# All four value tiles of a chunk in one stretch, with the global rows' sums in front of it

## The chip, the core and the metric

The kernel runs on one core of a Trainium2 chip. The metric is the device time of one execution in microseconds (us). The engines have short names here: PE is TensorE (matmuls), DVE VectorE, ACT ScalarE, POOL GpSimd, SP SyncE. The last one only issues DMAs in this kernel.

## The reference

A Longformer attention (a window of 32 positions on either side, and 8 global positions that see all and are seen by all) over 8 batches, 8 heads, 576 positions and 64 dimensions, and behind it a gated GELU block with a residual gate:

```python
scores = scale * np.matmul(q, k.transpose(0, 1, 3, 2))
mask = np.abs(pos[:, None] - pos[None, :]) <= 32
mask = mask | is_global[:, None] | is_global[None, :]
attn = softmax(np.where(mask, scores, -1e9))
x = np.matmul(attn, v)                 # to (4608, 512)
ffn_out = gelu(x @ w_gate) * (x @ w_val) @ w_out
return x + sigmoid(x @ w_res) * ffn_out
```

## The kernel before

The 4608 tokens are worked on in nine chunks of 512 (`c` = 0 to 8), each of eight windows of 64 queries, or four tiles of 128 tokens (`t` = 0 to 3). While chunk c goes through the gated block, chunk c+1's attention is made between its matmuls, so that PE always has work. The order is written by hand: each engine executes its instructions in the order in which the program gives them, and waits where an operand or a buffer is not ready.

For a chunk, `ffn_in` makes the 12 hidden tiles (`g_ps`, `v_ps`, `ht`). Behind them stand 16 work items, `work_f`: for each of the four token tiles a gate (`r_ps`, four matmuls, then a tanh into `rsb` on ACT) and three thirds of the output product (`f_ps`, four matmuls each). After the last third, DVE makes `prb` from `rsb` and `f_ps`, POOL adds the tokens (`ob`), and SP stores `ob`. The pieces of the next chunk's attention are hung in front of numbered work items, in `jobs`:

- `half(0)` and `half(1)` (job 0 and 3) make the scores `sc` of four windows each. ACT takes the exponentials into `pt`. The mask, a product of two bf16 tiles in SBUF (`pt` and `maskw`, line 565), is made on DVE in four instructions per half by `held_mask`.
- `global_rows` (job 3, in chunks whose successor brings a new batch, `held`) sums the global rows into the PSUM tile `sn`. DVE multiplies it by `head8` into `vgs` (line 520).
- `two(0)` and `two(2)` (job 4 and 8) make the values of two tiles: `local_values` (32 matmuls of 65 columns with 64 columns of the array, line 583), `global_values` (two matmuls per tile, each on 64 rows of the array, which read `vgs`, line 596), the normalizing on DVE (`norm`, a reciprocal and a product per tile or half tile), and `turn_x`, which for chunks above 1 is a DMA transpose from `xtok` to `xt` on SP. The next chunk's matmuls read `xt`.

PSUM has eight banks: four in the pool `psm` (`g_ps`, `v_ps`, `r_ps`, `f_ps`, the second scores), two in `pss` (the first scores), and one pair in `psn`, which is used in turn by the global scores, `sn` and a value tile. A tile that gets a bank waits until the last reader of the tile before has finished with it.

Of the kernel before, what the change touches and what calls it, by code (L numbers as in the profile page):

```python
# [8 lines left out]
F32 = mybir.dt.float32  # L9
# [4 lines left out]
ALU = mybir.AluOpType  # L14


def view(t, p0, pn, off, dims):

    step = t.ap[0][0]
    return bass.AP(tensor=t.tensor, offset=t.offset + p0 * step + off, ap=[[step, pn]] + dims)  # L20
# [3 lines left out]
def kernel(  # L24
# [12 lines left out]
    nc = tc.nc  # L37
    B, H, S, D = q.shape
# [8 lines left out]
    NW = S // 64  # L47
    CH = 8
    NCH = B * NW // CH
    NQT = 5  # L50
    VG = D + 1
    HV = 4 * VG
# [4 lines left out]
    work = ctx.enter_context(tc.tile_pool(name="work", bufs=2))  # L57
    psm = ctx.enter_context(tc.tile_pool(name="psm", bufs=4, space=bass.MemoryType.PSUM))
    pss = ctx.enter_context(tc.tile_pool(name="pss", bufs=2, space=bass.MemoryType.PSUM))
    psn = ctx.enter_context(tc.tile_pool(name="psn", bufs=1, space=bass.MemoryType.PSUM))  # L60
    ctx.enter_context(tc.manual_schedule())

    def pair_of(shape, name, dt=BF16):
        return [const.tile(shape, dt, name=f"{name}{i}", tag=f"{name}{i}") for i in range(2)]
# [7 lines left out]
    ve = [t.rearrange("p (c h e) -> p c h e", h=H, e=VG) for t in ve_flat]  # L72
    vo = [t.rearrange("p (c h e) -> p c h e", h=H, e=VG) for t in vo_flat]
    gt = pair_of([128, S + 128], "gt")
    ptg = pair_of([128, 5, 64], "ptg")
    xt = pair_of([128, NKT, 512], "xt")
    xtok = pair_of([128, 4, 512], "xtok")
    pt = const.tile([128, H, CH, 64], BF16, name="pt", tag="pt")
    vgs = const.tile([128, 2, H * VG], BF16, name="vgs", tag="vgs")
# [423 lines left out]
    def global_rows(b):  # L503

        e = b % 2
        if b:
            sn = psn.tile([128, 2, 512], F32, name="sn", tag="nd")[:, 0, 0:2 * VG]
        else:
            sn = pss.tile([128, 2 * VG], F32, name="sn", tag="sc")
        for c in range(-1, 5):  # L510
            for p in range(NP):
                if c < 0:
                    nc.tensor.matmul(sn[32 * p:32 * p + 32, :], own[e][:, 32 * p:32 * p + 32],
                                     view(vgb, 0, 128, (b // 2) * VG, [[0, 2], [1, VG]]), start=True, stop=False)
                else:
                    nc.tensor.matmul(sn[32 * p:32 * p + 16, :], ptg[e][:, c, 16 * p:16 * p + 16],
                                     ve[e][:, c, 2 * p:2 * p + 2, :], start=False, stop=(c == 4))
        n = NP if b else NP // 2
        for p in range(0, NP, n):
            nc.vector.tensor_tensor(view(vgs, 0, 128, e * H * VG + 2 * VG * p, [[2 * VG, n], [VG, 2], [1, VG]]),  # L520
                                    view(sn, 0, 128, 0, [[0, n], [VG, 2], [1, VG]]),
                                    view(head8, 0, 128, 2 * p, [[2, n], [1, 2], [0, VG]]), ALU.mult)
# [27 lines left out]
    def scores(c, quad, pps=(0, 1), between=None):  # L550

        i0 = (CH * c + 4 * quad) % NW
        banks = []
        for pp in pps:
            pool, tag = (psm, "mm") if pp else (pss, "sc")
            sc = [pool.tile([128, 2, 4, 64], F32, name="sc", tag=tag) for _ in range(2)]
            heads(c, quad, pp, sc, True)
            banks += [(pp, u, sc[u]) for u in range(2)]
        if between:
            between()  # L560
        mine = [weigh(quad, *which, stay=(c == 1)) for which in banks]

        def mask(n0, n1):
            for m, x in mine[n0:n1]:
                nc.vector.tensor_tensor(m, x, view(maskw, 0, 128, 64 * i0, [[0, 2], [64, 4], [1, 64]]), ALU.mult)  # L565
        return mask

    def split(c, t):
        return c == 0 and t % 2 == 0 or c > 1 and t % 2 == 1

    def local_values(c, t):
        if split(c, t):
            pool, tag = (pss, "sc") if c else (psm, "mm")
            nds = [pool.tile([128, 512], F32, name=f"nd{hf}", tag=tag) for hf in range(2)]
            nd = None
        else:
            nd = psn.tile([128, 2, 512], F32, name="nd", tag="nd")
            nds = [nd[:, 0, :], nd[:, 1, :]]
        wins = [divmod(CH * c + 2 * t + e, NW) for e in range(2)]
        for h in range(H):  # L580
            for e, (b, i) in enumerate(wins):
                vw = ve[b % 2][:, i // 2, h, :] if i % 2 == 0 else vo[b % 2][:, i // 2, h, :]
                nc.tensor.matmul(nds[h // 4][64 * e:64 * e + 64, VG * (h % 4):VG * (h % 4) + VG],  # L583
                                 pt[:, h, 2 * t + e, :], vw, start=(h % 4 == 0), stop=False)
        return nd, nds, wins

    def global_values(c, t, begun):
        nd, nds, wins = begun
        if wins[0][0] == wins[1][0]:
            parts = [(wins[0][0], 64 + 64 * wins[0][1])]  # L590
        else:
            parts = [(wins[0][0], S), (wins[1][0], 0)]
        for n, (b, c0) in enumerate(parts):
            for hf in range(2):
                k0, k1 = (64 * hf, 64 * hf + 64) if c > 1 else (0, 128)
                nc.tensor.matmul(nds[hf][:, 0:HV], gt[b % 2][k0:k1, c0:c0 + 128],  # L596
                                 vgs[k0:k1, b % 2, HV * hf:HV * hf + HV], start=False, stop=(n == len(parts) - 1))

    def values(c, t, begun=None):
        begun = begun or local_values(c, t)  # L600
# [3 lines left out]
    def norm(c, t, begun):  # L604
        nd, nds, wins = begun
        rden = work.tile([128, H], F32, name="rden", tag="rden")
        if split(c, t):
            for hf in range(2):
                num = nds[hf][:, 0:HV].rearrange("p (h e) -> p h e", e=VG)
                nc.vector.reciprocal(rden[:, 4 * hf:4 * hf + 4], num[:, :, D])  # L610
                nc.vector.tensor_tensor(xtok[c % 2][:, t, 256 * hf:256 * hf + 256].rearrange("p (h d) -> p h d", d=D),  # L611
                                        num[:, :, 0:D], view(rden, 0, 128, 4 * hf, [[1, 4], [0, D]]), ALU.mult)
            return
        num = nd[:, :, 0:HV].rearrange("p a (h e) -> p a h e", e=VG)
        r2 = rden.rearrange("p (a h) -> p a h", a=2)
        nc.vector.reciprocal(r2, num[:, :, :, D])
        nc.vector.tensor_tensor(xtok[c % 2][:, t, :].rearrange("p (a h d) -> p a h d", a=2, d=D),  # L617
                                num[:, :, :, 0:D], view(rden, 0, 128, 0, [[4, 2], [1, 4], [0, D]]), ALU.mult)

    def turn_x(c, t):  # L620
        mine = xt[c % 2][:, :, 128 * t:128 * t + 128]
        if c > 1:
            nc.sync.dma_start(mine, xtok[c % 2][:, t, :], transpose=True)
            return
        tx = pss.tile([128, NKT, 128], BF16, name="tx", tag="sc")
        for kk in range(NKT):
            nc.tensor.transpose(tx[:, kk, :], xtok[c % 2][:, t, 128 * kk:128 * kk + 128], ident)
        (nc.vector.tensor_copy if c or t == 3 else nc.scalar.copy)(mine, tx)
# [195 lines left out]
    for c in range(NCH):  # L824
        b = c + 1
# [5 lines left out]
        held = None  # L831
        for j in range(NFF):
# [54 lines left out]
            elif b < B:  # L887
# [15 lines left out]
                if j == 11:  # L903
                    held = global_scores(b)
        work_f = [w for t in range(4) for w in ffn_out(c, t)]
# [46 lines left out]
            continue  # L952
        jobs = {n: [] for n in range(16)}
        if c + 1 < NCH:
            if held is not None:
                jobs[3].append(lambda: global_rows(b))
            held_mask = {}

            def half(quad, between=None):
                held_mask[quad] = scores(c + 1, quad, between=between)  # L960

            jobs[0].append(lambda: half(0, held and (lambda: global_exp(b, *held))))
            jobs[1] += [gates[-1][1], lambda: held_mask[0](0, 4)]
            jobs[3].append(lambda: half(1))

            def two(t0):
                both = [local_values(c + 1, t) for t in (t0, t0 + 1)]
                for t in (t0, t0 + 1):
                    global_values(c + 1, t, both[t - t0])
                for t in (t0, t0 + 1):  # L970
                    norm(c + 1, t, both[t - t0])
                    turn_x(c + 1, t)

            jobs[4].append(lambda: two(0))
            jobs[8].append(lambda: two(2))
            jobs[5].append(lambda: held_mask[1](0, 2))
            jobs[6].append(lambda: held_mask[1](2, 4))
        for n in range(16):
            for w in jobs[n]:
                w()  # L980
# [33 lines left out]
```

## Time and profile before

| | |
|---|---|
| time, median of 3 runs | 385.8 us (385.33 to 386.08) |
| the profiled execution | 385.43 us |
| its span, first to last instruction | 383.7 us |
| PE busy | 370.2 us, 96% |
| DVE busy | 200.7 us, 52% |
| ACT busy | 169.6 us, 44% |
| POOL busy | 168.9 us, 44% |
| granted clock of PE | 1.00 |

The span leaves out what lies around the program, 1.7 us here. Busy times are added over instructions, and PE's matmuls overlap, so its 96% says only that it is seldom idle for long.

### The profile page before, as it was taken

How to read it: one execution, taken by the hardware profiler on the slowest of the kernel's cores; microseconds unless marked ns; L12 is line 12 of the kernel's file. 1: busy time of each engine (PE TensorE's matmuls, PEld its weight loads, DVE VectorE, ACT ScalarE, POOL GpSimd, SP SyncE). 2: the span in 40 equal slices, each digit the busy share in tenths (PEclk: the TensorE clock that was granted, in tenths of full speed). 3: DMA queues.
4: the chain of work that ended last, by engine and by line, in shares of the span. 5: the costliest groups of instructions: out<-in, count | busy, mean ns of one | idle time of the engine just before them, and what ended most of it. 6: DMA issues, size and time to landing. Idle time of an engine off the chain costs nothing.

```text
span 383.7 us, 8470 instructions
## 1 busy us (share of the span) xinstructions
PE 370.2 (96%) x3332; PEld 185.1 (48%) x3332; DVE 200.7 (52%) x467; ACT 169.6 (44%) x291; POOL 168.9 (44%) x203
## 2 busy tenths in 40 slices
PE   3989989999999999999999999999999999999996
PEld 2574555445544554455444544454445444444444
DVE  7767674536723573447434744564446534553322
ACT  4763685336333543355334633372338233723311
POOL 7877683868255624661366128712501210121012
PEclk9999999999999999999999999999999999999999
DMA  8999999799949943999399939994990410041002
GB/s 242 251 375 365 246 334 219 165 179 162 106 112 148 202 72 104 129 193 106 92 141 172 125 98 127 188 97 126 105 165 4 109 57 0 3 113 53 0 29 83
DMA packets 156810, 53.70 MB, mean 140 GB/s; under 512 B 140194, under 2 KB 147234, under 8 KB 156770
## 3 DMA queue, kind: packets, MB, share of 16 engines
q1 hardware_dynamic: 80832, 42.80, 46.8%
q0 software_dynamic: 75392, 9.84, 43.9%
q8 instruction: 26, 0.43, 0.5%
q10 hardware_dynamic: 546, 0.52, 0.4%
q14 instruction: 14, 0.11, 0.1%
HBM read 39.19 MB, written 9.44 MB: 127 GB/s over the span
## 4 chain that ended last, share of the span: by engine, by line
PE 84%; DMA 9%; SPq 3%; POOL 2%; issue 1%; DVE 0%; ACTq 0%; DVEq 0%; POOLq 0%
PE f_ps L703 24%; PE v_ps L647 22%; PE g_ps L647 22%; PE r_ps L673 8%; DMA extra<-in_moe_w_val_dram 5%; PE nd L583 3%; SPq L185 3%; PE sc L540 2%; DMA wo_t<-in_k_dram 2%; PE nd L596 2%; DMA xtok<-in_v_dram 2%; DMA ht<-in_q_dram 1%; POOL wo_t L145 1%; PE sg L478 1%; PE sg L485 1%
## 5 line engine op out<-in xcount | busy, mean ns | idle before, releaser
L656 DVE SCALAR_TENSOR_TENSOR ht<-gsb,v_ps 128x512 bf16<-128x512 bf16 x108 | 74.2, 688 | 97.5 <-PE v_ps L647 90.2
L653 ACT ACTIVATE gsb<-g_ps 128x512 bf16<-128x512 f32 x108 | 64.4, 597 | 121.9 <-PE g_ps L647 120.7
L709 POOL TENSOR_TENSOR ob<-prb,xtok 128x512 f32<-128x512 f32 x35 | 40.3, 1155 | 167.0 <-DVE prb L707 167.0
L647 PE MATMUL g_ps<-xt,wg_t 128*128 128x512 bf16 (+1 forms) x456 | 111.9, 368 | 0.0
L647 PE MATMUL v_ps<-xt,wv_t 128*128 128x512 bf16 (+1 forms) x456 | 111.9, 368 | 0.0
L703 PE MATMUL f_ps<-wo_t,ht 128*128 128x512 bf16 x420 | 97.9, 379 | 0.0
L647 PEld LDWEIGHTS <-wv_t 128*128 128x128 bf16 x456 | 43.5, 98 | 49.1
L647 PEld LDWEIGHTS <-wg_t 128*128 128x128 bf16 x456 | 43.4, 98 | 48.7
L703 PEld LDWEIGHTS <-ht 128*128 128x128 bf16 x420 | 40.4, 98 | 46.9
L681 ACT ACTIVATE rsb<-r_ps 128x512 bf16<-128x512 f32 x36 | 21.9, 611 | 66.5 <-PE r_ps L673 66.5
L707 DVE SCALAR_TENSOR_TENSOR prb<-rsb,f_ps 128x512 f32<-128x512 bf16 x35 | 24.1, 688 | 51.2 <-PE f_ps L703 50.4
L673 PE MATMUL r_ps<-wr_t,xt 128*128 128x512 bf16 x144 | 37.0, 381 | 1.0 <-ACT rsb L681 1.0
L547 ACT ACTIVATE pt<-sc 128x512 bf16<-128x512 f32 x64 | 33.3, 615 | 3.8 <-PE sc L540 3.8
L91 POOL DMA_DIRECT2D q_st<-in_q_dram x25 | 21.5, 866 | 18.2 <-DMA qt<-q_st 18.1
L99 POOL DMA_DIRECT2D ve<-in_v_dram x30 | 25.5, 866 | 0.0
L565 DVE TENSOR_TENSOR pt<-pt,maskw 128x512 bf16<-128x512 bf16 x56 | 21.9, 422 | 2.5 <-ACT pt L547 0.9
L91 POOL DMA_DIRECT2D k_st<-in_k_dram x25 | 21.2, 867 | 3.6 <-DMA kt<-k_st 2.9
L673 PEld LDWEIGHTS <-xt 128*128 128x128 bf16 x144 | 12.3, 98 | 15.8 <-issue 3.9
L583 PEld LDWEIGHTS <-pt 128*64 128x64 bf16 x576 | 11.2, 110 | 9.7 <-issue 5.0
L583 PE MATMUL nd<-ve,pt 128*64 128x65 bf16 x320 | 13.6, 196 | 0.7 <-DVE xtok L617 0.6
L617 DVE TENSOR_TENSOR xtok<-nd,rden 128x512 bf16<-128x512 f32 x20 | 13.8, 691 | 0.8
L611 DVE TENSOR_TENSOR xtok<-nd,rden 128x256 bf16<-128x256 f32 x32 | 13.6, 425 | 1.1
(174 smaller groups left out, 289.4 us busy)
## 6 DMA issues: line engine op xcount, KB each, us to landing
out_dram<-ob SPq DMA_DIRECT2D x35, 256.0 KB
vo<-ve SPq DMA_DIRECT2D x12, 260.0 KB
q_st<-in_q_dram POOLq DMA_DIRECT2D x20, 128.0 KB, 6.3
k_st<-in_k_dram POOLq DMA_DIRECT2D x20, 128.0 KB, 6.7
ve<-in_v_dram POOLq DMA_DIRECT2D x18, 128.0 KB, 7.6
wo_t<-in_k_dram SPq DMA_DIRECT2D x8, 256.0 KB
vraw<-in_q_dram SPq DMA_DIRECT2D x8, 256.0 KB
extra<-in_moe_w_out_dram SPq DMA_DIRECT2D x4, 512.0 KB
```

The lines of the kernel that those rows point to most:

```text
L91: nc.gpsimd.dma_start(dst[0:n, r, :].rearrange("p (h d) -> p h d", d=D), src[b].rearrange("h s d -> s h d")[128 * r:128 * r + n])
L99: nc.gpsimd.dma_start(t[p0:p1, c, :, 0:D], v[b].rearrange("h s d -> s h d")[s0 + p0:s0 + p1])
L547: nc.scalar.activation(sc if stay else mine, sc, ACTF.Exp, bias=0.0, scale=SCALE)
L565: nc.vector.tensor_tensor(m, x, view(maskw, 0, 128, 64 * i0, [[0, 2], [64, 4], [1, 64]]), ALU.mult)
L583: nc.tensor.matmul(nds[h // 4][64 * e:64 * e + 64, VG * (h % 4):VG * (h % 4) + VG], pt[:, h, 2 * t + e, :], vw, start=(h % 4 == 0), stop=F ...
L647: nc.tensor.matmul(held[what][:, c0:c1], w[:, kk, 128 * j:128 * j + 128], x[:, kk, c0:c1], start=(kk == 0), stop=(kk == NKT - 1))
L653: nc.scalar.activation(held["s"], held["g"], ACTF.Gelu, bias=0.0, scale=1.0)
L656: nc.vector.scalar_tensor_tensor(ht[:, j, :], held["s"], 0.5, held["v"], ALU.mult, ALU.mult)
L673: nc.tensor.matmul(r_ps, xt[c % 2][:, kk, 128 * t:128 * t + 128], wr_t[:, kk, :], start=(kk == 0), stop=(kk == NKT - 1))
L703: nc.tensor.matmul(held["f"], ht[:, j, 128 * t:128 * t + 128], wo_t[:, j, :], start=(j == 0), stop=(j == NFF - 1))
L707: nc.vector.scalar_tensor_tensor(prb, held["r"], 1.0, held["f"], ALU.add, ALU.mult)
L709: nc.gpsimd.tensor_tensor(ob, prb, xtok[c % 2][:, t, :], ALU.add)
```

## The change

In chunks 2 to 8 the values of all four tiles are made in one stretch, `all_values`, in front of work item 6. It uses six banks: `outer` (the `pss` pair) for tile 0, `middle` (two of `psm`) for tile 1, and `inner` (the `psn` pair) for tile 2 and three heads of each half of tile 3. The fourth head of each half of tile 3 goes to the free columns of `outer`. First come the 64 local matmuls of all tiles, then the global ones, then all the normalizing and the four transposes. `global_rows` moves from job 3 to the front of this stretch. The third gate moves from item 8 to item 5. All four masks of the second half are made in job 4, in front of the second gate.

```diff
     def split(c, t):
-        return c == 0 and t % 2 == 0 or c > 1 and t % 2 == 1
+        return c == 0 and t % 2 == 0
...
+    def all_values(c, before=None):
+
+        if before:
+            before()
+        HH = H // 2
+        H3 = HH - 1
+        outer = [pss.tile([128, 512], F32, name=f"nd0{hf}", tag="sc") for hf in range(2)]
+        middle = [psm.tile([128, 512], F32, name=f"nd1{hf}", tag="mm") for hf in range(2)]
+        inner = psn.tile([128, 2, 512], F32, name="nd2", tag="nd")
+
+        def places(t, hf):
+            if t < 3:
+                return [((outer, middle)[t][hf] if t < 2 else inner[:, hf, :], 0, 0, HH)]
+            return [(inner[:, hf, :], HV, 0, H3), (outer[hf], HV, H3, HH)]
+
+        for t in range(4):
+            for h in range(H):
+                hf, n = divmod(h, HH)
+                bank, o, h0 = [(bank, o, h0) for bank, o, h0, h1 in places(t, hf) if h0 <= n < h1][0]
+                o += VG * (n - h0)
+                for e in range(2):
+                    b, i = divmod(CH * c + 2 * t + e, NW)
+                    vw = ve[b % 2][:, i // 2, h, :] if i % 2 == 0 else vo[b % 2][:, i // 2, h, :]
+                    nc.tensor.matmul(bank[64 * e:64 * e + 64, o:o + VG], pt[:, h, 2 * t + e, :], vw,
+                                     start=(n == 0 and t < 3), stop=False)
+        for t in range(4):
+            (b, i), (b2, _) = (divmod(CH * c + 2 * t + e, NW) for e in range(2))
+            parts = [(b, 64 + 64 * i)] if b == b2 else [(b, S), (b2, 0)]
+            for n, (b, c0) in enumerate(parts):
+                for part in range(len(places(t, 0))):
+                    for hf in range(2):
+                        bank, o, h0, h1 = places(t, hf)[part]
+                        k0 = 64 * hf
+                        nc.tensor.matmul(bank[:, o:o + VG * (h1 - h0)], gt[b % 2][k0:k0 + 64, c0:c0 + 128],
+                                         vgs[k0:k0 + 64, b % 2, HV * hf + VG * h0:HV * hf + VG * h1],
+                                         start=False, stop=(t in (1, 3) and n == len(parts) - 1))
+
+        def divide(num, dst, a, n):
+            rden = work.tile([128, H], F32, name="rden", tag="rden")
+            r = rden[:, 0:a * n].rearrange("p (a h) -> p a h", h=n)
+            nc.vector.reciprocal(r, num[:, :, :, D])
+            nc.vector.tensor_tensor(dst, num[:, :, :, 0:D], view(rden, 0, 128, 0, [[n, a], [1, n], [0, D]]), ALU.mult)
...
+        for t in range(4):
+            if t == 2:
+                both(0, 0, HH, 2)
+            elif t == 3:
+                both(HV, 0, H3, 3)
+            for hf in range(2):
+                for bank, o, h0, h1 in places(t, hf):
+                    if t != 2 and (t < 3 or h0):
+                        divide(bank[:, o:o + VG * (h1 - h0)].rearrange("p (a h e) -> p a h e", a=1, e=VG),
...
+            turn_x(c, t)
...
         if c + 1 < NCH:
-            if held is not None:
-                jobs[3].append(lambda: global_rows(b))
+            work_f[5:9] = [work_f[8]] + work_f[5:8]
...
-            def two(t0):
-                both = [local_values(c + 1, t) for t in (t0, t0 + 1)]
-                for t in (t0, t0 + 1):
-                    global_values(c + 1, t, both[t - t0])
-                for t in (t0, t0 + 1):
-                    norm(c + 1, t, both[t - t0])
-                    turn_x(c + 1, t)
-
-            jobs[4].append(lambda: two(0))
-            jobs[8].append(lambda: two(2))
-            jobs[5].append(lambda: held_mask[1](0, 2))
-            jobs[6].append(lambda: held_mask[1](2, 4))
+            jobs[4].append(lambda: held_mask[1](0, 4))
+            jobs[6].append(lambda: all_values(c + 1, held and (lambda: global_rows(b))))
```

Three places show how instructions move. The first is DVE's order while chunk 3's attention is made, before the change, from the first half's masks on (`x4` are four such instructions, and in brackets stand the engines that an instruction waits for):

```order
L565 TENSOR_TENSOR pt<-pt,maskw 128x2x256 [waits Activation_49] x4
L520 TENSOR_TENSOR vgs<-sn,head_169 128x520 [waits PE_49]
L707 SCALAR_TENSOR_TENSOR prb<-rsb,f_ps 128x512 [waits PE_49,Activation_49,Pool_49]
L616 RECIPROCAL rden<-nd 128x8 [waits PE_49]
L617 TENSOR_TENSOR xtok_89<-nd,rden 128x512 [waits DVE_49]
L610 RECIPROCAL rden<-nd_2306 128x4 [waits PE_49]
L611 TENSOR_TENSOR xtok_89<-nd_2306,rden 128x256 [waits DVE_49]
```

Behind these come the second half tile's reciprocal and product, and only then the second half's four masks. DVE's order at the same place in the changed kernel:

```order
L565 TENSOR_TENSOR pt<-pt,maskw 128x2x256 [waits Activation_49] x4
L765 SCALAR_TENSOR_TENSOR prb<-rsb,f_ps 128x512 [waits PE_49,Activation_49,Pool_49]
L565 TENSOR_TENSOR pt<-pt,maskw 128x2x256 [waits Activation_49] x4
L520 TENSOR_TENSOR vgs<-sn,head_169 128x520 [waits PE_49]
L637 RECIPROCAL rden<-nd_2316 128x4 [waits PE_49]
L638 TENSOR_TENSOR xtok_89<-nd_2316,rden 128x256 [waits DVE_49]
```

The second half's masks have moved up to stand directly behind `prb`, and `vgs` has moved behind them.

The second place is PE's order in the changed kernel, around the start of chunk 2's stretch (`nd00` and `nd01` are `outer`, `nd10` is half of `middle`, `nd2` is `inner`; one row stands for each run of like matmuls):

```order
L731 MATMUL r_ps_1734<-wr_t_96,xt1_87 128x512
L731 MATMUL r_ps_1741<-wr_t_96,xt1_87 128x512
L513 MATMUL sn_1748<-vgb_232,own0_214 32x130
L516 MATMUL sn_1748<-ve0_78,ptg0_84 16x130
L620 MATMUL nd00_1774<-ve1_79,pt_90 64x65
L620 MATMUL nd10_1776<-vo0_80,pt_90 64x65
L620 MATMUL nd2_1778<-ve0_78,pt_90 64x65 [waits DVE_49]
L630 MATMUL nd00_1774<-vgs_91,gt1_83 128x260
L630 MATMUL nd2_1778<-vgs_91,gt0_82 128x195
L761 MATMUL f_ps_1881<-wo_t_95,ht_92 128x512
```

`sn` and the first matmul into `nd2`, which waits for DVE, now have only tile 0's and tile 1's 32 local matmuls between them; before, 32 score matmuls and four of `f_ps` stood there.

The third place is SP's DMA queue from the stores of chunk c's tile 0 on, before the change:

```order
L711 DMA out_dram<-ob 128x512
L623 DMA_TRANSPOSE xt_86<-xtok_88 128x4x128 x2
L711 DMA out_dram<-ob 128x512
L623 DMA_TRANSPOSE xt_86<-xtok_88 128x4x128 x2
L711 DMA out_dram<-ob 128x512 x2
```

and in the changed kernel:

```order
L769 DMA out_dram<-ob 128x512
L681 DMA_TRANSPOSE xt_86<-xtok_88 128x4x128 x4
L769 DMA out_dram<-ob 128x512 x3
```

The four transposes now stand together, ahead of tile 1's store.

## Rows read from the trace of the kernel before

**Rows 1.** Page, busy time, share and instructions of PE and others.
```profile
PE 370.2 (96%) x3332; PEld 185.1 (48%) x3332; DVE 200.7 (52%) x467; ACT 169.6 (44%) x291; POOL 168.9 (44%) x203
```

**Rows 2.** Timeline of PE, 249 to 270 us: start, length, line, tiles, count.
```profile
253.75 0.24 PE L513 MATMUL sn<-vgb,own 128*32 128x130 bf16 x4
253.82 0.46 PE L516 MATMUL sn<-ve,ptg 128*16 128x130 bf16 x20
254.21 0.64 PE L540 MATMUL sc<-qt,kt 64*128 64x64 bf16 x32
254.78 1.04 PE L703 MATMUL f_ps<-wo_t,ht 128*128 128x512 bf16 x4
255.75 0.22 PE L583 MATMUL nd<-vo,pt 128*64 128x65 bf16 x1
...
256.38 0.40 PE L596 MATMUL nd<-vgs,gt 64*128 64x260 bf16 x4
256.71 1.04 PE L673 MATMUL r_ps<-wr_t,xt 128*128 128x512 bf16 x4
257.59 2.75 PE L703 MATMUL f_ps<-wo_t,ht 128*128 128x512 bf16 x12
260.27 0.22 PE L583 MATMUL nd<-vo,pt 128*64 128x65 bf16 x1
...
262.11 2.75 PE L703 MATMUL f_ps<-wo_t,ht 128*128 128x512 bf16 x12
...
268.16 1.03 PE L647 MATMUL g_ps<-xt,wg_t 128*128 128x512 bf16 x4
```

**Rows 3.** Windows, early: length, then busy time by engine, PEclk, DMA.
```profile
52.50:54.00 1.50, 0.53 (x25) 0.41 (x18) 1.25 (x3) 1.50 (x4) 1.39 (x3) 1.00 1.04 389
```

**Rows 4.** Timeline of DVE in the same chunk.
```profile
251.86 0.46 DVE L501 TENSOR_TENSOR gt<-gt,maskr 128x576 bf16<-128x576 bf16 x1 [1.36 <-ACT gt L500]
...
254.33 0.70 DVE L520 TENSOR_TENSOR vgs<-sn,head 128x520 bf16<-128x520 f32 x1
255.95 0.69 DVE L707 SCALAR_TENSOR_TENSOR prb<-rsb,f_ps 128x512 f32<-128x512 bf16 x1 [0.93 <-PE f_ps L703]
...
258.11 0.17 DVE L610 RECIPROCAL rden<-nd 128x4 f32<-128x4 f32 x1
...
258.66 1.42 DVE L565 TENSOR_TENSOR pt<-pt,maskw 128x512 bf16<-128x512 bf16 x4
```

**Rows 5.** Timeline of DVE near the kernel's start.
```profile
16.16 0.42 DVE L765 COPY vo<-ve 64x1040 bf16<-64x1040 bf16 x1
...
18.65 1.12 DVE L501 TENSOR_TENSOR gt<-gt,maskr 128x576 bf16<-128x576 bf16 x1
19.99 0.76 DVE L520 TENSOR_TENSOR vgs<-sn,head 128x260 bf16<-128x260 f32 x2 [0.22 <-PE sn L516]
```

**Rows 6.** Timeline of PE there, with its releaser.
```profile
20.47 0.72 PE L596 MATMUL nd<-vgs,gt 128*128 128x260 bf16 x3 [0.53 <-DVE vgs L520]
```

**Rows 7.** Groups by line and shape: count, busy us, mean ns, idle.
```profile
L520 DVE TENSOR_TENSOR vgs<-sn,head 128x260 bf16<-128x260 f32 x2 | 0.8, 422 | 0.2 <-PE sn L516 0.2
...
L267 POOL CAST k_st<-wo_t 128x512 bf16<-128x512 f32 x2 | 1.2, 618 | 0.0
```

**Rows 8.** Timeline of ACT in the same chunk.
```profile
254.65 2.07 ACT L547 ACTIVATE pt<-sc 128x512 bf16<-128x512 f32 x4 [0.36 <-PE sc L540]
```

**Rows 9.** Timeline of POOL in the same chunk.
```profile
256.73 1.15 POOL L709 TENSOR_TENSOR ob<-prb,xtok 128x512 f32<-128x512 f32 x1 [6.89 <-DVE prb L707]
```

**Rows 10.** Timeline of POOL near the kernel's start.
```profile
16.37 0.69 POOL L190 CAST ve<-vraw 128x512 bf16<-128x512 f32 x1 [0.27 <-DMA vraw<-in_v_dram]
...
18.30 1.16 POOL L774 COPY vo<-ve 64x1040 bf16<-64x1040 bf16 x1
```

**Rows 11.** Timeline of SyncE's DMA queue in the same chunk.
```profile
262.88 2.53 SPq L623 DMA_TRANSPOSE xt<-xtok  x2
```

**Rows 12.** Timeline of PE in chunk 2's first values.
```profile
98.05 0.19 PE L583 MATMUL nd<-vo,pt 128*64 128x65 bf16 x1 [0.32 <-issue]
```

More of the change, by code (lines that the diff above doesn't have):

```diff
@@ L568, in split @@
     def split(c, t):
-        return c == 0 and t % 2 == 0 or c > 1 and t % 2 == 1
+        return c == 0 and t % 2 == 0
     def local_values(c, t):
         if split(c, t):
-            pool, tag = (pss, "sc") if c else (psm, "mm")
-            nds = [pool.tile([128, 512], F32, name=f"nd{hf}", tag=tag) for hf in range(2)]
+            nds = [psm.tile([128, 512], F32, name=f"nd{hf}", tag="mm") for hf in range(2)]
             nd = None
@@ L594, in global_values, with both @@
             for hf in range(2):
-                k0, k1 = (64 * hf, 64 * hf + 64) if c > 1 else (0, 128)
-                nc.tensor.matmul(nds[hf][:, 0:HV], gt[b % 2][k0:k1, c0:c0 + 128],
-                                 vgs[k0:k1, b % 2, HV * hf:HV * hf + HV], start=False, stop=(n == len(parts) - 1))
+                nc.tensor.matmul(nds[hf][:, 0:HV], gt[b % 2][:, c0:c0 + 128],
+                                 vgs[:, b % 2, HV * hf:HV * hf + HV], start=False, stop=(n == len(parts) - 1))
+    def all_values(c, before=None):
[36 more added lines that the diff above has]
+            nc.vector.tensor_tensor(dst, num[:, :, :, 0:D], view(rden, 0, 128, 0, [[n, a], [1, n], [0, D]]), ALU.mult)
+        def both(o, h0, h1, t):
+            divide(inner[:, :, o:o + VG * (h1 - h0)].rearrange("p a (h e) -> p a h e", e=VG),
+                   xtok[c % 2][:, t, :].rearrange("p (a h d) -> p a h d", a=2, d=D)[:, :, h0:h1, :], 2, h1 - h0)
+        for t in range(4):
[7 more added lines that the diff above has]
+                        divide(bank[:, o:o + VG * (h1 - h0)].rearrange("p (a h e) -> p a h e", a=1, e=VG),
+                               xtok[c % 2][:, t, :].rearrange("p (a h d) -> p a h d", a=2, d=D)[:, hf:hf + 1, h0:h1, :],
+                               1, h1 - h0)
+            turn_x(c, t)
```

## The prediction

> **What bounds the kernel now.** I read the page's busy shares first, and there TensorE (PE) is busy for 96% of the span [rows 1]. A busy share does not say that the engine works back to back, so I then went through one chunk's matmuls in order of time, in the stretch where chunk 6's attention is made between chunk 5's output products [rows 2]. The reader is to see that each group starts when the one before has streamed through. From 262.11 to 268.16, 28 matmuls of 512 columns take 6.05 us, 0.216 us each; so 4 take 0.86 and 12 take 2.59. Wherever the shape of the array changes (128\*128, 64\*128, 128\*64, 128\*32), the step is longer: 12 matmuls before the values take 257.59 to 260.27, 2.68, which is 0.09 more than 2.59, and the four gate matmuls that follow a change take 256.71 to 257.59, 0.88, another 0.01 to 0.02. I take 0.09 for a change and 0.01 for the slower restart. There is no other idle time in this stretch, so PE sets the end, and the question for each edit is what PE streams, how often it changes shape, and for whom it waits. The granted clock is 1.00 (the 2.4 GHz level), and it stayed so through a stretch of 1.5 us in which PE was busy for only 0.53 us [rows 3]; a wait of about 1 us should cost its own length and nothing for the clock.
>
> **The change, part by part.** All times below are counted from 253.75 in that chunk, which ends at 268.16, after 14.41 us.
>
> *PE without any wait.* Before, the order is sn, scores, f, values, gate, f, values, gate, f and so on. After, it is scores, f, two gates, sn, all values, f and so on. From the rows: scores to f 0.57 (254.21 to 254.78), four f matmuls behind a change 0.88, the two gates 0.86 each, one change 0.09, so sn begins at 3.26 and its larger part at 3.33. From there to the next shape is 0.39 (253.82 to 254.21), so the values begin at 3.72. 32 value matmuls and a change take 0.63 (255.75 to 256.38), so 32 alone take 0.54: tile 2 could begin at 4.26 and the global matmuls at 4.89. Two pairs of global matmuls and a change take 0.33 (256.38 to 256.71), so 0.12 a pair: three pairs 0.36, the fourth tile's four narrower ones with the same 520 columns 0.13, a change 0.09, which gives 5.47. Twelve f matmuls behind a change 2.60, then the unchanged 6.05: the chunk ends at 14.12. That is 0.29 us less than 14.41, the worth of three changes of shape, and seven chunks have it: 2.0 us. The two extra matmuls per chunk are in it.
>
> *The wait for the global rows' sums.* The new `inner` tile (value tiles 2 and 3) lies in the same bank pair as sn, so its first matmul waits until VectorE (DVE) has read sn into vgs. In this chunk vgs starts 0.51 after the larger part of sn (253.82 to 254.33) and takes 0.70 [rows 2, 4]. From DVE's end to PE's start I count 0.05: two vgs pieces begin at 19.99, the first lasts 0.42, and the waiting matmul starts at 20.47 [rows 5 to 7]. So vgs could end at 3.33 + 0.51 + 0.70 = 4.54 and PE go on at 4.59, not 4.26: 0.33 us in each of the six chunks that have new global rows. This alone eats the gain (-0.29 + 0.33 = +0.04 a chunk). Before, scores and f lay between sn and the next use of that bank, and nothing waited.
>
> *The masks.* This is where I expect the time to go. The four mask multiplications of the second half now stand directly behind prb, the product that ends tile 0's f. Before, four normalizing operations stood between, and the masks ran as 4 in 1.42 us (each 0.42 long, a new one each 0.33) at 258.66, long after ScalarE's exponentials (2.07 us, begun 0.44 after the scores) [rows 4, 8]. After, prb starts 1.17 behind f's start (254.78 to 255.95), so at 0.57 + 1.17 = 1.74, and ends at 2.43; the first mask starts 0.09 before that end, at 2.34, and ends at 2.76. The exponentials start near 0.44 and are done by 2.6, so they don't hold the masks up. Undisturbed, the masks end at 3.76, just in time for vgs at 3.84.
>
> But prb also releases GpSimd's (POOL) sum ob, 0.78 after prb's start (255.95 to 256.73), which takes 1.15 us [rows 9]: at 2.52, in the middle of the first mask. Before, ob ran beside the normalizing, which reads PSUM. The trace shows what a DVE product of two bf16 tiles in SBUF does beside a POOL operation: `gt*maskr` takes 0.46 at 251.86 [rows 4] but 1.12 at 18.65, where a POOL copy ran from 18.30 to 19.46; it ended 0.31 after that copy, so in effect it began 0.15 before the copy's end [rows 5, 10]. The reverse is there too: a POOL cast issued at 16.37 during a DVE copy (16.16 to 16.58) took 0.69 against 0.62 for its shape [rows 7], so it began 0.14 before DVE's end, ahead of DVE's next operation. By these rows ob begins at 2.76 - 0.14 = 2.62 and ends at 3.77, the second mask begins at 3.62 and ends at 4.04, the fourth ends at 4.70, vgs starts at 4.61 and ends at 5.31, and PE goes on at 5.36 instead of 4.26. That is 1.10 of waiting: +0.81 us in each of six chunks. Chunk 8 has no sn; there tile 2 could begin at 3.80 and waits for the fourth mask until 4.75: +0.66.
>
> The Trainium skill, "SBUF — State Buffer", section "Who interferes with whom", says that a DVE instruction with two SBUF inputs and a GpSimd instruction that reads SBUF exclude each other, and that whichever issues first keeps the port for its whole instruction. The trace agrees that one blocks the other, but shows an overlap of 0.14 and 0.15 us at the ends; without it, by the page, the masks would end 0.29 later and the time be 7 x 0.29 = 2.0 us longer, 393.0. I take the rows' value.
>
> *Costed at nothing.* The third gate's earlier place: it uses a bank that an exponential of the second scores has freed long before. DVE's normalizing in one burst: each half tile takes 0.55 (258.11 to 258.66), so the burst is at most 9 x 0.55 = 5.0 us, hidden under the 8.65 us of f and gate matmuls that follow the stretch; tile 1's prb comes later by that, and nothing in the chunk waits for it. The four transposes on SyncE's queue are a rival below.
>
> **Sum.** 6 x 0.81 + 0.66 = 5.5 us. The profiled execution took 385.43, so 390.9; it lies 0.37 below the median of the three runs shown (385.8), within their scatter of 0.75. I write 391.0.
>
> **The rivals.**
> *A, DVE keeps the port.* If ob has to wait until the four masks are through, the masks end at 3.76 and only the 0.33 wait stays: 6 x 0.04 - 0.28 (chunk 8, whose masks are then ready 0.01 late) = about 0, 385.4. For it: the masks follow each other closely, with no semaphore between, and no row shows POOL and the next DVE operation both asking at once. Against it: in the row at 16.37 POOL got in before DVE's next operation.
> *C, the lock bites in part.* If ob holds up the masks for half of the 0.78 us that I count (5.36 - 4.59 = 0.77 on PE), 6 x 0.43 + 0.2 = 2.8: 388.2.
> *W, the transposes are late too.* Tile 3's DMA transpose was issued 262.88 + 1.27 = 264.15, 4.0 us before the next chunk's first matmul [rows 2, 11]. After, it stands behind the burst, up to 0.2 + 5.0 us behind the stretch's end, with 8.65 us to go: 3.45 left. If a transpose needs the full 4.0, PE waits up to 0.55 in seven chunks: 3.9 on top, 394.8. No row shows a wait for it, so the need may be far less.
> *F, faster.* If vgs came before tile 2 is due, no wait at all: 7 x 0.29 = 2.0 gained, 383.4. It decides at 4.26: vgs would have to end 0.28 us earlier than the 0.51 + 0.70 of the rows, and ob must not disturb the masks. A smaller gain is a hole of 0.32 us in PE at 98.05, in chunk 2's first values, for which the trace names no releaser [rows 12]; it may go or stay, and I leave it in.
>
> **How the numbers follow.** The port's case 0.70, A 0.14, C 0.06, W 0.06, F 0.04. The likeliest gives 391.0, by itself 390.3 to 392.2 (the hole gone; vgs or the masks 0.2 us later in each chunk). The range 385.2 to 392.4 takes in A, C and nearly all of the likeliest; W, F and the page's value are left out. A measurement of this kernel tells about 0.2%, 0.77 us, from no change: faster 0.05 (F, and a little of A), same 0.13 (the rest of A), slower 0.82.
>
> **What would show it.** In the changed kernel's profile: three changes of shape fewer per chunk; a PE wait of about 1.1 us before tile 2's first value matmul, released by DVE's vgs, in six chunks, and by a mask in the seventh; among the last three of the four masks behind prb one that takes over 1 us instead of 0.42; ob of tile 0 beginning inside the first mask. If the masks all take 0.42 and ob is long instead, A holds and the wait is 0.33. Wrong altogether would be a wait in front of the first value matmuls, or one at the next chunk's first matmul, which would be W.

## The result, and the profile after

The changed kernel takes 391.7 us (median of five runs, 390.77 to 392.08) and the kernel before 385.9 (five runs beside it, 385.33 to 386.08): a ratio of 1.0137, 95% interval 1.0110 to 1.0164. By the ratio it is slower by 5.3 us, by the two medians by 5.8, and the forecast was 391.0.

The page's busy times and the group of the masks, in the profiled execution of 391.75 us (columns of the group: busy us, mean ns of one, idle time ahead of it):

```profile
PE 370.2 (95%) x3348; PEld 187.6 (48%) x3348; DVE 211.9 (54%) x495; ACT 169.3 (43%) x291; POOL 169.4 (43%) x203
...
L565 DVE TENSOR_TENSOR pt<-pt,maskw 128x512 bf16<-128x512 bf16 x56 | 28.6, 540 | 2.5 <-ACT pt L547 0.9
```

PE is busy for as long as before [rows 1], so the added time is time in which it waits. DVE gained 11 us, and 6.7 of them are in the 56 masks, which the change only moves: they took 21.9 us before, a mean of 422 ns, and 28.6 now.

Now the chunk of [rows 2] in the changed kernel, PE's timeline:

```profile
257.81 0.64 PE L540 MATMUL sc<-qt,kt 64*128 64x64 bf16 x32
258.39 1.04 PE L761 MATMUL f_ps<-wo_t,ht 128*128 128x512 bf16 x4
259.26 1.89 PE L731 MATMUL r_ps<-wr_t,xt 128*128 128x512 bf16 x8
261.08 0.24 PE L513 MATMUL sn<-vgb,own 128*32 128x130 bf16 x4
261.15 0.45 PE L516 MATMUL sn<-ve,ptg 128*16 128x130 bf16 x20
261.53 0.22 PE L620 MATMUL nd<-vo,pt 128*64 128x65 bf16 x1
...
262.05 0.19 PE L620 MATMUL nd<-ve,pt 128*64 128x65 bf16 x1
263.21 0.19 PE L620 MATMUL nd<-vo,pt 128*64 128x65 bf16 x1 [0.97 <-DVE vgs L520]
...
263.85 0.62 PE L630 MATMUL nd<-vgs,gt 64*128 64x260 bf16 x10
264.41 5.35 PE L761 MATMUL f_ps<-wo_t,ht 128*128 128x512 bf16 x24
...
273.05 1.03 PE L705 MATMUL g_ps<-xt,wg_t 128*128 128x512 bf16 x4
```

Tile 1's last local matmul starts at 262.05 and tile 2's first at 263.21. That is 1.16 where a step is 0.03 (tile 2's rows go on at 263.24), so PE waits 1.13 us, for vgs. DVE and POOL in the same place, then PE's waits over the whole span (us in total, times, longest):

```profile
259.56 0.69 DVE L765 SCALAR_TENSOR_TENSOR prb<-rsb,f_ps 128x512 f32<-128x512 bf16 x1 [1.25 <-PE f_ps L761]
260.16 0.42 DVE L565 TENSOR_TENSOR pt<-pt,maskw 128x512 bf16<-128x512 bf16 x1
...
260.16 1.71 DVE L565 TENSOR_TENSOR pt<-pt,maskw 128x512 bf16<-128x512 bf16 x2
...
260.16 2.38 DVE L565 TENSOR_TENSOR pt<-pt,maskw 128x512 bf16<-128x512 bf16 x4
262.47 0.68 DVE L520 TENSOR_TENSOR vgs<-sn,head 128x520 bf16<-128x520 f32 x1
```
```profile
260.33 1.26 POOL L767 TENSOR_TENSOR ob<-prb,xtok 128x512 f32<-128x512 f32 x1 [6.43 <-DVE prb L765]
```
```profile
PE nd L620 <- DVE vgs L520: 5.8, 6, 1.0
```

The first mask takes 0.42 and ends at 260.58; both first masks together take 1.71, so the second ends at 261.87; all four take 2.38 where they took 1.42 [rows 4]. POOL's ob was issued at 260.33, inside the first mask, and ended at 261.59. With the 1.15 that it takes alone [rows 9] it began at 260.44, 0.14 before the first mask's end, and the second mask, 0.42 long, began at 261.45, 0.14 before ob's end. The six waits are the six chunks with new global rows. Chunks (from one chunk's first `g_ps` to the next one's) last 40.28 us instead of 39.45, and the last one 38.66 instead of 38.04: +0.83 and +0.62, where the forecast was +0.81 and +0.66.

### The profile page after: what moved, and what is told of

Read it like the earlier page. It is cut to its first block, busy times and chain, and to the rows that moved or that the text cites. A ratio compares the mean times of both kernels' runs of the same rounds, so it can differ in the third digit from the quotient of the medians.

```text
span 390.1 us, 8535 instructions
## 1 busy us (share of the span) xinstructions
PE 370.2 (95%) x3348; PEld 187.6 (48%) x3348; DVE 211.9 (54%) x495; ACT 169.3 (43%) x291; POOL 169.4 (43%) x203
## 4 chain that ended last, share of the span: by engine, by line
PE 77%; DMA 10%; DVE 7%; SPq 3%; POOL 1%; issue 1%; ACTq 0%; DVEq 0%; POOLq 0%
PE f_ps L761 24%; PE g_ps L705 21%; PE v_ps L705 21%; PE r_ps L731 4%; DVE pt L565 4%; DMA qt<-in_moe_w_val_dram 2%; DMA wo_t<-in_k_dram 2%; PE sc L540 2%; DMA extra<-in_moe_w_res_dram 2%; DMA vraw<-in_moe_w_out_dram 2%; SPq L185 1%; DMA ht<-in_q_dram 1%; SPq L142 1%; DVE prb L765 1%; PE nd L620 1%; PE nd L630 1%
## 5 line engine op out<-in xcount | busy, mean ns | idle before, releaser
L761 PE MATMUL f_ps<-wo_t,ht 128*128 128x512 bf16 x420 | 96.8, 379 | 0.0
L739 ACT ACTIVATE rsb<-r_ps 128x512 bf16<-128x512 f32 x36 | 21.9, 612 | 74.3 <-PE r_ps L731 74.2
L731 PE MATMUL r_ps<-wr_t,xt 128*128 128x512 bf16 x144 | 35.7, 380 | 1.0 <-ACT rsb L739 1.0
L565 DVE TENSOR_TENSOR pt<-pt,maskw 128x512 bf16<-128x512 bf16 x56 | 28.6, 540 | 2.5 <-ACT pt L547 0.9
L638 DVE TENSOR_TENSOR xtok<-nd,rden 128x256 bf16<-128x256 f32 (+3 forms) x56 | 23.8, 424 | 2.3
L731 PEld LDWEIGHTS <-xt 128*128 128x128 bf16 x144 | 13.4, 98 | 16.1 <-issue 0.9
L637 DVE RECIPROCAL rden<-nd 128x4 f32<-128x4 f32 (+3 forms) x56 | 9.7, 174 | 9.7 <-PE nd L630 9.7
L540 PEld LDWEIGHTS <-kt 64*128 64x128 bf16 x576 | 10.0, 96 | 8.9 <-issue 8.1
L620 PE MATMUL nd<-ve,pt 128*64 128x65 bf16 x248 | 10.2, 195 | 3.9 <-DVE vgs L520 3.9
```

The lines of the kernel that those rows point to most:

```text
L638: nc.vector.tensor_tensor(dst, num[:, :, :, 0:D], view(rden, 0, 128, 0, [[n, a], [1, n], [0, D]]), ALU.mult)
L731: nc.tensor.matmul(r_ps, xt[c % 2][:, kk, 128 * t:128 * t + 128], wr_t[:, kk, :], start=(kk == 0), stop=(kk == NKT - 1))
L761: nc.tensor.matmul(held["f"], ht[:, j, 128 * t:128 * t + 128], wo_t[:, j, :], start=(j == 0), stop=(j == NFF - 1))
```

## The experiments

All are timed against the kernel before on the same chip. "Chunk" is the length of a regular chunk, "last" that of the chunk beside which chunk 8's attention is made, "wait" PE's wait in front of or among tile 2's local matmuls in a regular chunk, all from the profiled executions.

| kernel | median us | ratio (95% interval) | chunk | last | wait |
|---|---|---|---|---|---|
| before | 385.4 to 385.9 | 1 | 39.45 | 38.04 | 0 |
| after | 391.7 | 1.0137 (1.0110 to 1.0164) | 40.28 | 38.66 | 1.13 |
| e1 masks ahead of prb | 385.93 | 1.0005 (0.9989 to 1.0020) | 39.48 | 38.05 | 0.33 |
| e2 sums back | 390.14 | 1.0117 (1.0094 to 1.0141) | 39.97 | 38.81 | 0.84 |
| e3 both | 383.61 | 0.9953 (0.9936 to 0.9971) | 39.13 | 37.72 | 0 |
| e4 before, masks up | 387.22 | 1.0043 (1.0030 to 1.0056) | 39.73 | 38.31 | (0.25, tile 3) |
| e5 ob twice | 400.84 | 1.0379 (1.0354 to 1.0404) | 41.24 | 39.69 | 2.10 |
| e6 gate back | 391.62 | 1.0155 (1.0134 to 1.0177) | 40.28 | 38.70 | 1.13 |
| e7 fourth gate | 387.25 | 1.0042 (1.0028 to 1.0056) | 39.55 | 38.57 | 0.33 |
| e9 stretch earlier | 398.79 | 1.0344 (1.0311 to 1.0377) | 41.15 | 39.42 | 2.00 |
| e10 ob on DVE | 386.32 | 1.0012 (0.9998 to 1.0027) | 39.48 | 37.79 | 0.33 |

In "last" there is also what the next chunk's first matmul waits for the transposes, counted as its step less the usual 0.22: 0.11 after the change, 0.33 in e1, 0.26 in e2, 0.18 in e5, 0.15 in e6, 0.86 in e7, 0.07 in e10, and nothing before the change and in e3, e4 and e9.

The theory that they test is the lock: POOL's ob holds up the masks, vgs stands behind them, and PE waits for vgs at the bank that tile 2 shares with sn. Its rivals were that DVE's queue alone makes vgs late, and that sharing the bank is the whole price.

**e1, the masks ahead of prb.**

```diff
-            jobs[4].append(lambda: held_mask[1](0, 4))
+            jobs[3].append(lambda: held_mask[1](0, 4))
```

> The changed kernel with the second half's masks one job earlier, ahead of tile 0's prb on DVE; nothing else moves. Lock theory (POOL's ob holds up the masks, and PE waits for what stands behind them): ob now starts behind the masks, each mask takes 0.42 us, vgs ends where the sums alone allow it, and PE waits 0.33 us a chunk in place of 1.13 in six chunks, 0 to 0.3 in the last one. A chunk of 39.45 before becomes 39.5; in all 385.5 us, 386.7 if the 1.2 us that the changed kernel lost ahead of its first chunk belong to the program. Queue theory (vgs is late because four masks and prb stand ahead of it on DVE, POOL or not): the same work stands ahead of it in another order, the wait stays 1.1 and the time 391.

DVE in the same chunk of this kernel:

```profile
255.46 1.90 DVE L565 TENSOR_TENSOR pt<-pt,maskw 128x512 bf16<-128x512 bf16 x4 [0.58 <-ACT pt L547]
257.27 0.68 DVE L765 SCALAR_TENSOR_TENSOR prb<-rsb,f_ps 128x512 f32<-128x512 bf16 x1
258.24 0.70 DVE L520 TENSOR_TENSOR vgs<-sn,head 128x520 bf16<-128x520 f32 x1 [0.28 <-PE sn L516]
```

The masks now follow ScalarE's exponentials (four in 1.90, each 0.42), vgs waits for the sums, not for DVE, and PE waits 0.33 us. The same work stands ahead of vgs on DVE, which speaks against the queue rival. It doesn't rule it out alone, since the masks now run in time in which DVE was idle; e10 keeps their place and does. The edit takes back 0.80 us a chunk.

**e2, the sums in front of the second scores again.**

```diff
+            if held is not None:
+                jobs[3].append(lambda: global_rows(b))
...
-            jobs[6].append(lambda: all_values(c + 1, held and (lambda: global_rows(b))))
+            jobs[6].append(lambda: all_values(c + 1))
```

> The changed kernel with the global rows' sums back in front of the second scores, so vgs is done long before the values; the masks stay behind prb. Lock theory: one mask still takes over 1.3 us, and PE waits for the last masks instead of vgs, 0.7 to 0.9 us a chunk; with the 0.29 saved in each of seven chunks this is 388.0 to 389.4 us. Bank theory (the whole price is that sn and the third value tile share a bank pair, so that PE waits for vgs): no wait is left, 383.4 to 384.2.

vgs is done at 258.69, long before the values; the masks are as slow as in the changed kernel (four in 2.39), and PE's 64 local matmuls take 0.84 us longer from first to last than in e3, in steps as mask after mask comes. The chunk is 39.97. So the bank is not the whole price, and either way out alone leaves the other wait. The time is 0.7 us above the forecast's upper end. In the profiled execution (390.88) the chunks are 4.1 us longer than before and the part ahead of chunk 1 1.4 us; on the latter see e8.

**e3, both edits.**

> The changed kernel with both: the masks ahead of tile 0's prb and the global rows' sums in front of the second scores. Lock theory with the bank's 0.33 beside it: every mask takes 0.42 us, no wait for vgs, at most 0.1 us a chunk for the bank that prb frees later; seven chunks are 0.2 to 0.3 us shorter than before, 383.4 to 384.2 us, ratio 0.994 to 0.997. If the three changes of shape are worth nothing, 385.4; queue theory says 385.4 or more, since DVE has the same work ahead of the values.

DVE in the same chunk:

```profile
253.71 0.70 DVE L520 TENSOR_TENSOR vgs<-sn,head 128x520 bf16<-128x520 f32 x1
254.66 1.89 DVE L565 TENSOR_TENSOR pt<-pt,maskw 128x512 bf16<-128x512 bf16 x4 [0.25 <-ACT pt L547]
256.46 0.68 DVE L765 SCALAR_TENSOR_TENSOR prb<-rsb,f_ps 128x512 f32<-128x512 bf16 x1
```

vgs and the masks are both done before PE reaches the values at 256.85, and nothing waits. The chunk is 39.13, 0.32 shorter than before, and the last one too (37.72 for 38.04): this is what one stretch in place of two is worth. The version is faster than both kernels, than the one before by 0.47%.

**e4, the kernel before with the masks behind prb.**

```diff
+            jobs[4].append(lambda: held_mask[1](0, 4))
             jobs[4].append(lambda: two(0))
             jobs[8].append(lambda: two(2))
-            jobs[5].append(lambda: held_mask[1](0, 2))
-            jobs[6].append(lambda: held_mask[1](2, 4))
```

> The kernel before with one edit: all four masks of the second half directly behind tile 0's prb, ahead of the normalizing. Lock theory: one mask takes over 1.3 us here as well, and DVE is busy about 1 us longer a chunk, but tile 2's values come only some 4 us behind that prb, so nothing waits: 385.4 to 386.2 us. If the longer masks cost time wherever they stand (or the normalizing behind them is then late for a bank), 0.8 us a chunk: 391.

The collision came, in a program without the change's stretch (mean of a mask 540 ns here too), but the expectation that nothing waits was wrong. The normalizing now stands behind the slow masks. Tile 1's second half is normalized only at 261.72, and tile 3's second half uses that bank:

```profile
261.49 0.19 PE L583 MATMUL nd<-vo,pt 128*64 128x65 bf16 x1
261.78 0.22 PE L583 MATMUL nd<-ve,pt 128*64 128x65 bf16 x1
```

A step of 0.29 in place of 0.03; the chunk is 0.28 longer. The same 0.96 us lost on DVE costs 0.28 here and 0.80 in the changed kernel: the price is set by where PE next needs DVE.

**e5, POOL's sum of tile 0 made twice** (the second writes the same values).

```diff
-                    nc.gpsimd.tensor_tensor(ob, prb, xtok[c % 2][:, t, :], ALU.add)
+                    for _ in range(2 if t == 0 and 0 < c < NCH - 1 else 1):
+                        nc.gpsimd.tensor_tensor(ob, prb, xtok[c % 2][:, t, :], ALU.add)
```

> The changed kernel with POOL making the sum ob of tile 0 twice in the chunks whose successor is prepared beside it (chunk 0, built in another way, stays); the second sum writes the same values. Lock theory, with the two engines taking turns: the first sum blocks the second mask, that mask gets in between, the second sum begins 0.14 us before its end and blocks the third mask by about 0.9 us; PE's wait grows from 1.13 to 2.0 us in six chunks and from 0.84 to 1.7 in the last, seven times 0.87 or 6.1 us more: 397 to 398.5 us, ratio to before 1.029 to 1.034. If POOL keeps the port for both sums, one mask takes 2.4 us and the price is about the same or 0.15 less. If POOL has no part in the wait: 391.7 us, 1.0137.

DVE, then POOL, in the same chunk, and the group of all masks:

```profile
265.52 3.35 DVE L565 TENSOR_TENSOR pt<-pt,maskw 128x512 bf16<-128x512 bf16 x4
268.80 0.69 DVE L520 TENSOR_TENSOR vgs<-sn,head 128x520 bf16<-128x520 f32 x1
```
```profile
265.69 2.56 POOL L768 TENSOR_TENSOR ob<-prb,xtok 128x512 f32<-128x512 f32 x2 [6.55 <-DVE prb L765]
```
```profile
L565 DVE TENSOR_TENSOR pt<-pt,maskw 128x512 bf16<-128x512 bf16 x56 | 35.3, 660 | 2.5 <-ACT pt L547 0.9
```

Two of the four masks are long (1.38 each, the second and the third), so the engines take turns; the four take 3.35, once more 0.97 longer, and so does the chunk (41.24 for 40.28, 0.09 more than I forecast). The masks' busy time is 6.7 us above that of the changed kernel, as that one's is above before. The rest of the miss is the clock. Two chunks lasted 42.9, 1.7 us more, and in this one PEclk fell behind the wait (columns: busy us of PE, PEld, DVE, ACT, POOL, then PEclk):

```profile
266.00:270.00 4.00, 2.07 (x88) 1.44 (x88) 3.48 (x4) 0.88 (x2) 2.18 (x2) 1.00 0.19 70
...
272.00:274.00 2.00, 2.00 (x6) 0.67 (x5) 1.90 (x8) 0.00 (x0) 0.00 (x0) 0.50 0.33 65
274.00:277.00 3.00, 3.00 (x15) 1.36 (x14) 1.82 (x7) 0.00 (x0) 0.94 (x1) 0.95 0.44 88
```

**e6, the third gate at its old place** (the line that moves it is taken out).

> The changed kernel with the third gate left at its old place, behind the stretch. Lock theory: the end of the masks and of vgs hangs on tile 0's prb and on POOL, not on the gate, so PE reaches the stretch 0.86 us earlier and waits for it 0.86 us longer for the masks; vgs, behind the masks, ends where it did. Seven chunks at up to 0.86: 6.0 us more, 397 to 398 us, ratio 1.029 to 1.032. If the gate's place is worth nothing: 391.7 us, 1.0137.

Nothing changed, and the expectation had the edit wrong: without that line a third of tile 1's output product, also four matmuls of 0.216 us, stands in front of the stretch instead of the gate. What stands there is of no account; this run doesn't show what its length is worth.

**e9, the length itself taken away**: e6 with `all_values` in job 5.

> The changed kernel with the third gate at its old place and the whole stretch one work item earlier, so that only one gate's four matmuls, 0.86 us, lie between tile 0's last output matmul and the sums in place of two groups. Putting back the gate alone changed nothing, since a third of tile 1's output product, of the same length, took its place; this run takes the length itself away. Lock theory: masks and vgs end where they did, PE arrives 0.86 us earlier and waits 1.99 us in six chunks, 1.7 in the last: 41.15 us a chunk in place of 40.28, 6.0 us more, 397 to 398 us, ratio 1.028 to 1.033; up to 1 us more in a chunk if the clock falls after so long a wait. If the price were the long mask itself, 391.6 us, 1.0155.

The chunk is 41.15 and PE waits 2.00 us: 0.87 longer, since masks and vgs end where they did. The ratio is a little above what was expected; one chunk lasted 42.84, and there too the granted clock fell to half behind the wait.

**e7, the fourth gate ahead of the stretch as well.**

```diff
-            work_f[5:9] = [work_f[8]] + work_f[5:8]
+            work_f[5:13] = [work_f[8], work_f[12]] + work_f[5:8] + work_f[9:12]
...
-            jobs[6].append(lambda: all_values(c + 1, held and (lambda: global_rows(b))))
+            jobs[7].append(lambda: all_values(c + 1, held and (lambda: global_rows(b))))
```

> The changed kernel with the fourth gate moved ahead of the stretch as well. The collision stays: one mask still takes 1.38 us. But PE now has 0.86 us more to do before the stretch. Lock theory: vgs starts when both the masks and the sums are done, about 4.70 us into the stretch instead of 4.61, and tile 2 is due at 5.12 instead of 4.26; PE waits 0.3 us for vgs in six chunks and about 0.1 in the last, so a chunk takes what it took before, 39.45 to 39.5: 385.4 to 386.2 us, ratio 0.999 to 1.002. If what costs is the long mask itself, wherever PE stands, 391.7 us.

The masks are as slow as in the changed kernel (mean 540 ns), and their price is gone: the wait is 0.33, the chunk 39.55. The time is 1.05 us above the forecast's upper end, and one part of that is the rival on the transposes. SyncE's queue and PE in the last of these chunks:

```profile
340.22 5.89 SPq L681 DMA_TRANSPOSE xt<-xtok  x4
```
```profile
347.50 1.02 PE L705 MATMUL g_ps<-xt,wg_t 128*128 128x512 bf16 x4 [0.70 <-DMA xt<-xtok]
```

With one gate less behind the stretch, the next chunk's first matmul waits for tile 3's transpose. Its step is 0.86 us above the usual 0.22 here (0.70 of that is the idle time in the row), and 0.09 in a regular chunk. In both it starts 1.4 us after the end of the four issues (346.11 and 347.50; 267.98 and 269.38). Over the seven chunks this makes some 1.4 us, and without it they would be shorter than before; as it is, they are 0.7 longer. The other part is what lies ahead of chunk 1: it took 1.15 us more than in the first profile of the kernel before; on that see e8.

**e10, tile 0's sum on DVE behind vgs.**

```diff
+    late = []
...
-                    nc.gpsimd.tensor_tensor(ob, prb, xtok[c % 2][:, t, :], ALU.add)
                     r0 = 512 * c + 128 * t
-                    nc.sync.dma_start(out[r0:r0 + 128, :], ob)
+                    def add(engine):
+                        engine.tensor_tensor(ob, prb, xtok[c % 2][:, t, :], ALU.add)
+                        nc.sync.dma_start(out[r0:r0 + 128, :], ob)
+                    if t == 0 and 0 < c < NCH - 1:
+                        late.append(add)
+                    else:
+                        add(nc.gpsimd)
...
+            def sums(b=b, held=held):
+                if held:
+                    global_rows(b)
+                late.pop()(nc.vector)
-            jobs[6].append(lambda: all_values(c + 1, held and (lambda: global_rows(b))))
+            jobs[6].append(lambda: all_values(c + 1, sums))
```

> The changed kernel with tile 0's sum ob, in the chunks whose successor is prepared beside it, made by DVE behind vgs (in the last of them behind the masks) instead of by POOL. The masks stay behind prb, the sums in front of the values. Lock theory: POOL does nothing while the masks run, each takes 0.42 us, vgs ends at 4.54 of the stretch and PE waits 0.33 us in six chunks and not at all in the last; the extra sum on DVE, about 1 us, fits into the 1.3 us that DVE is idle between vgs and the first reciprocal: a chunk takes 39.5, in all 385.4 to 386.3 us, ratio 0.999 to 1.002. If the masks are long for another reason than POOL (their place behind prb, or what ACT or PE do then), 391 us or more.

```profile
255.83 0.69 DVE L766 SCALAR_TENSOR_TENSOR prb<-rsb,f_ps 128x512 f32<-128x512 bf16 x1 [1.25 <-PE f_ps L762]
256.44 1.42 DVE L565 TENSOR_TENSOR pt<-pt,maskw 128x512 bf16<-128x512 bf16 x4
257.93 0.70 DVE L520 TENSOR_TENSOR vgs<-sn,head 128x520 bf16<-128x520 f32 x1
258.55 0.68 DVE L771 TENSOR_TENSOR ob<-prb,xtok 128x512 f32<-128x512 f32 x1
```

These are DVE's rows. The masks stand where the change put them, directly behind prb, and with POOL idle beside them they take 1.42 again. PE's wait is 0.33. This is the cleanest proof of the cause: place, sums and burst are the changed kernel's, and only POOL's sum is gone from beside the masks (on DVE it takes 0.68 us, behind vgs).

**e8, the changed kernel once more.**

> The changed kernel once more, for its stretch ahead of the first chunk, which ended 1.2 us later than in the kernel before although no code differs there. If that is chance, the first output of chunk 1's hidden products starts near 70.4 us this time and the run takes about 390.7 us; if it belongs to the program, 71.6 and 391.7 again.

Chunk 1's first `g_ps` came at 70.65 and the run took 390.79; in the first profile it came at 71.62, before the change at 70.41. Over all twelve profiled executions it lies between 70.1 and 71.8, and no code ahead of it differs. Most of that is chance. One piece may not be: PE's first matmul waits until 3.94 in both executions of the changed kernel and in e5 and e7, and until 3.5 in the others. Where these 0.46 us come from stays open.

## Why the prediction was right

- **PE without waits** (-0.29 a chunk): e3, where nothing waits, shows -0.32.
- **The wait for the sums** (0.33): e1, e7 and e10 show 0.33, from a row of the kernel's start and one chunk's distance of vgs to sn.
- **The masks.** ob was to begin 0.14 before the first mask's end and the second mask 0.15 before ob's end, which made a wait of 1.10 on PE; measured are 0.14, 0.14 and 1.13. (Between prb and the masks stood six normalizing operations before, not four; no term uses the count.) e10 shows that POOL is the cause, e5 that a second such sum costs the same again (0.97), e7 and e9 that 0.86 us more or less of work ahead of the stretch turn into that much less or more of waiting (0.80, down to the 0.33 of the sums, and 0.87). The page "SBUF — State Buffer" of the Trainium skill (section "Who interferes with whom") is borne out in what it says of the exclusion; its hold for the whole instruction would, by an estimate with the two 0.14 of the rows, have made the masks end 0.28 us later than they did, so there the measurement decides.
- **The last chunk** (+0.66): +0.62, but by luck so near, since two errors cancel. The fourth mask was to hold up all of tile 2's local matmuls, for 0.95 us. PE went on mask by mask instead, in three steps among tile 2's matmuls, and the 64 local matmuls take only 0.83 us longer from first to last than in e3 (1.87 for 1.04). Another 0.11 us, which the sum has at nothing, is a wait for the transposes: the 12 matmuls ahead of the next chunk's first one take 2.70 us (349.30 to 352.00 below) where 12 without a wait take 2.59.
- **Costed at nothing.** The third gate's place: right, but only since a group of equal length would stand there otherwise (e6). The normalizing burst lasts from 264.52 to 269.06, 4.5 us (bound: 5.0), and no regular chunk waits for what is behind it. The margin was thinner than I had it: in the changed kernel's last of these chunks the issues end at 350.60 and the next matmul starts at 352.00, the 1.4 us that e7 shows to be needed, and that is the wait of 0.11. One of the four transposes takes 2.07 us there, where each takes 1.21 to 1.22 in the regular chunk; why, the runs don't show. In the regular chunk the last issue starts at 269.66 and takes 1.21 (the four end at 270.87, the row below), or 3.39 before 273.05; 3.45 were foretold for rival W. In e7 it starts at 266.76, so the need is 269.38 - 266.76 = 2.62, not 4.0; that is why W came in the changed kernel's last chunk alone, and with 0.11.
- **The sum.** The seven chunks are 5.1 us longer together, where 5.5 was forecast: six regular ones give 5.0 by the table's lengths and the last 0.6, and the hole that I left in (0.51 from matmul to matmul in chunk 2 before) is gone. With e8's start that is 390.8, with the first profile's 391.8. Between forecast and median lie only that start and the hole. So how near the total came, 391.7 for 391.0, is in part chance: the start alone moves a run by up to 1.7 us (70.1 to 71.8).
- **The rivals.** A (DVE keeps the port) fell with the second mask, which ends only at 261.87, C with the 0.14, F with the 0.33 that even e1 and e10 leave.

SyncE's queue in the changed kernel, the four transposes of the regular chunk and those of the last one, and PE at the end of the last one:

```profile
265.73 5.14 SPq L681 DMA_TRANSPOSE xt<-xtok  x4
...
344.59 6.01 SPq L681 DMA_TRANSPOSE xt<-xtok  x4
```
```profile
349.30 2.75 PE L761 MATMUL f_ps<-wo_t,ht 128*128 128x512 bf16 x12
352.00 1.02 PE L705 MATMUL g_ps<-xt,wg_t 128*128 128x512 bf16 x4
```

## What to carry to other kernels

When instructions move on DVE, look at what POOL does at the new place: a DVE product of two SBUF tiles and a POOL sum of two SBUF tiles ran one after the other here, and the delay (0.96 us) fell on whichever engine next needed DVE. Price such a delay there and not where it arises: the same collision cost 0.80, 0.28 or nothing, by what PE had still to do before it needed the result. Where two waits end at nearly the same matmul (masks and vgs here), removing one only uncovers the other: of the 0.83 us a chunk, e1 took back 0.80 and e2 0.31, and only both together gave the gain of the merged stretch.

## What was not expected of the hardware

- The granted clock fell after some waits of about 2 us. Behind none of the waits of 1.13 (the changed kernel, e6, e8) did it fall; behind 2.1 us (e5) two chunks of six, and behind 2.0 (e9) one of six, ran for some microseconds at 0.50, the 1.2 GHz level, where a matmul of 512 columns takes 0.43 instead of 0.216, and lost 1.7 us. Why these and not the others, the runs don't tell.
- With both engines having work ready, they alternated instruction by instruction in e5 (1.38 us for the second and the third mask): a waiting POOL sum got in between two DVE products that follow each other closely, and a DVE product between two POOL sums.
- Single holes of 0.4 to 1.0 us in PE come at different places in different programs (97.5 before, with no releaser; 170.6 in e1, until a DMA of `kt` had landed; 89.2 in e2, until DVE had made `qgd`). Each was read in one profiled execution, so one of them shouldn't be taken for a part of an edit's price.
